# The first scores of one attention pair two products later, and the exponentials' tables loaded behind the last silu

## The chip, the cores and the metric

The kernel runs on one core of a Trainium2 chip. Its engines work side by side, each through its own list of instructions in order: TensorE (PE, matrix products into PSUM), VectorE (DVE), ScalarE (ACT), GpSimd (POOL), and SyncE (SP), which here issues the DMA transfers. The metric is the device time of one execution in microseconds (us); lower is better.

## The reference

An attention layer feeds a SwiGLU feed-forward layer, all in float32. There are 8 batches, 12 heads, 448 tokens and 64 features a head.

```python
def rmsnorm(x, g):
    rms = np.sqrt(np.mean(x * x, axis=-1, keepdims=True) + 1e-06)
    return x / rms * g
q_n, k_n = (rmsnorm(q, g_q), rmsnorm(k, g_k))
scores = scale * np.matmul(q_n, k_n.transpose(0, 1, 3, 2))   # scale = 1 / sqrt(64)
scores = scores - np.max(scores, axis=-1, keepdims=True)
attn = np.exp(scores)
attn = attn / (np.sum(attn, axis=-1, keepdims=True) + 1e-09)
attn = np.matmul(attn, v)
# heads side by side: x is 3584 tokens x 768
g = x @ w_gate                                # 768 x 1536
silu = g * (1.0 / (1.0 + np.exp(-g)))
out = (silu * (x @ w_val)) @ w_out            # 1536 x 768
```

## The kernel before, in words

**Tiling.** Attention is worked in 48 pairs of heads (`attention(m)`, m from 0 to 47). The feed-forward layer is worked in four blocks (`block(n)`, n from 0 to 3), each for two batches, that is, for twelve pairs. Pairs 0 to 11 come before block 0 (`EARLY` is 12). The later twelve of a group are interleaved with the block before them: pair 12 begins near the end of block 0's up stage, and pairs 12 to 23 fill the gaps of its down stage.

**A block.** The up stage makes `x @ w_gate` and `x @ w_val`. The matrices are cut in three by three pieces and multiplied with fifteen products (x0 to x14) of sums of pieces. Each step of the up stage is a product for the gate (w0, into a PSUM bank called `mm`) and one for the value (w1, into a bank called `at`), line L1472. Each bank has to be read (L1408, L1410, L1412, L1414: a copy on ACT or an addition or subtraction on DVE) before TensorE writes it again two products later. L1526 (`add_d`) is one more addition after x0. When a result of the gate is complete, ACT takes its silu (L1549), and DVE weighs the value with it (L1552). Lines L1184 and L1188 (`combined`) form sums of hidden pieces on DVE. The down stage (L1655) multiplies with `w_out` in the same manner.

**A pair.** Queries and keys are loaded (L768), squared on ACT (L807), summed on DVE (L838), and their inverse root is found by a logarithm and an exponential (L707, L708) with three small DVE steps (L713 to L715). POOL scales them (L888), DVE transposes them (L922), and ACT writes the queries with the gains (L925); a pair's scores can start after that. The scores (L970) come in four parts j: parts 0, 1 and 2 cover 896 columns, as two heads of 448, part 3 half as many. They go in the order 3, 0, 1, 2, into a ring of two PSUM banks called `st`, which the silus and the denominators share. Each part has its exponential on ACT (L985: tiles `es` for 0 to 2, `more` for 3). POOL adds the exponentials of 0 and 1 and then of 2 (L990); DVE adds part 3 (L996). PE multiplies the exponentials with the values (L1048) and sums them to a denominator (L1079); L1123 to L1151 turn that into a division.

**Order.** No engine chooses its order at run time. A planner (`Order`) takes pieces of work with `add(engine, us, when, emit, after, takes, uses, group, mode, early, rank)`. It plays the execution with assumed durations and writes out the instructions in the order in which it starts the pieces. `when` less `rank` is a piece's due time, by which pieces of one engine are sorted; `after` names pieces that must have ended; `takes` and `uses` name tiles in rings. `early`, if given, forbids a start earlier than `when - early`. On an engine, a piece that could start more than 0.4 us ahead of the one that is due goes first. A changed piece therefore can move other pieces, on any engine, for as long as the plan takes to fall into its old order.

**Tables.** ACT holds the table for one set of functions at a time. A piece with `mode="logarithms"` or `mode="silu"` is of one of two sets. When the planner starts a piece of another mode than the last piece with a mode on that engine, it adds 1.3 us to the plan; for logarithms (which include the exponentials) it also calls `load_tables` (L572), so that the load is written ahead of that piece. The load for the silus (shown at L1549) is put ahead of the first silu that needs it.

Of the kernel before, what the change touches and what calls it, by code (L numbers as in the profile page):

```python
# [364 lines left out]
class Order:  # L365
# [28 lines left out]
    def add(  # L394
        self, engine, us, when, emit, after=(), takes=(), uses=(), port=False, moves=(), group=None,
        mode=None, early=None, rank=0.0,
    ):
        piece = dict(
            engine=engine, us=us, when=when, emit=emit, takes=takes, port=port, moves=moves,
            group=group, mode=mode, early=early, rank=rank,  # L400
            after=[a for a in after if a is not None], end=None, n=len(self.pieces),
        )
        for tile_of in (*takes, *uses):
            self.users.setdefault(tile_of, []).append(piece)
        self.pieces.append(piece)
        return piece
# [87 lines left out]
def fast(  # L494
# [53 lines left out]
    NB = B // 2  # L548
# [5 lines left out]
    EARLY = 2 * NPAIR  # L554
# [116 lines left out]
    def block_start(n):  # L671
        return FIRST + n * (UP + BOTH) + MORE * (n > 0)

    def block_end(n):
        return block_start(n) + UP + MORE * (n == 0)

    def pair_time(m):
        if m < EARLY:
            return LEAD + m * PAIR, PAIR
        n, i = divmod(m - EARLY, EARLY)  # L680
        return block_end(n) + (i - 1) * BOTH / EARLY, BOTH / EARLY
# [54 lines left out]
    def attention(m):  # L736
# [8 lines left out]
        base, span = pair_time(m)  # L745

        ready = base - span
        early = m < EARLY
        rank = 60.0 if early else 0.0

        def add(*what, **more):
            return order.add(*what, rank=rank, **more)
# [31 lines left out]
        def load_values():  # L784
# [10 lines left out]
            early=4.0 if early else 25.0,  # L795
# [14 lines left out]
        for x in range(2):  # L810
# [4 lines left out]
                    after=[loaded[x], *squares, clusters.get("estimate") if m == 1 else None], uses=[("qk", (m, x))] + [("t", m)] * x,  # L815
# [41 lines left out]
        for x in range(2 if m < 2 else 0):  # L857
            sums = add(
                "DVE", 0.65, ready - 17.0, lambda x=x: summed_half(x),
                after=[squares[x], sums, clusters.get("turned") if x else None],  # L860
# [4 lines left out]
            after=squares, uses=[("t", m)], takes=[("ss", m)]  # L865
# [10 lines left out]
        def scale(x):  # L876
            if natural:
# [18 lines left out]
                after=[rr], port=True,  # L896
# [34 lines left out]
        if natural:  # L931
            of_turned = ("st", (m, "turned"))
            for xs_of in ((1, 0),) if m == 0 else ((1,), (0,)):
                qt = add(
                    "PE", 0.4 * len(xs_of), ready - 6.0, lambda xs_of=xs_of: [turn(x) for x in xs_of],
                    after=[scaled[1 - xs_of[-1]], qt], mode="full",
# [25 lines left out]
        def scores(j):  # L962
            st = take("st", (m, j), [P, 2, TB])
            n = S * width(j) // P
            for x in range(2):

                of_keys, of_queries = (x, 0) if j < NJ - 1 else (0, x)
                for h in range(2):
                    rows = ds(D * h, D)
                    nc.tensor.matmul(  # L970
                        st[ds(D * x, D), h, 0:n],
                        tiles["KT", m][rows, ds(P * j + D * of_keys, D)],
                        tiles["QT", m][rows, ds(Q * of_queries, n)],
                        start=True,
                        stop=True,
                    )


        def weights_of(j):
            return ("ea" if early else "e", (m, j)) if j < NJ - 1 else ("eh", m)  # L980

        def exps(j):
            e = take(*weights_of(j), [P, 2, S if j < NJ - 1 else Q])
            tiles["e", (m, j)] = e
            nc.scalar.activation(e, tiles["st", (m, j)][:, :, 0 : S * width(j) // P], AF.Exp)  # L985

        def add_up(j):
            to, e = tiles["sums", m], tiles["e", (m, j)]
            if j < NJ - 1:
                nc.gpsimd.tensor_tensor(  # L990
                    out=to, in0=tiles["e", (m, 0)] if j == 1 else to, in1=e, op=ALU.add
                )
            else:
                for x in range(2):
                    part = to[ds(D * x, D), :, ts(x, Q)]
                    nc.vector.tensor_tensor(out=part, in0=part, in1=e[ds(D * x, D)], op=ALU.add)  # L996
# [3 lines left out]
        ex, adds = {}, []  # L1000
        for j in (3, 0, 1, 2):
            before = clusters.get((m - 2, "weighted" if j in (3, 0) else "total"))
            when = (ready + 0.3 if j in (3, 0) else base) + 0.01 * (j % 3)
            half = j == NJ - 1
            st = add(
                "PE", 0.38 if half else 0.75, when, lambda j=j: scores(j),
                after=[kt, qt, staged.get(ES), before],
                uses=[("KT", m), ("QT", m)], takes=[("st", (m, j))],
                group=("c", m - 1 if j in (3, 0) else m), mode="quarters",
            )  # L1010
            ex[j] = add(
                "ACT", 0.54 if half else 0.92, when + 1.0, lambda j=j: exps(j),
                after=[st], uses=[("st", (m, j))],
                takes=[weights_of(j)], mode="logarithms",
            )
            if j in (1, 2) and not early:

                def more_sums(j=j):
                    if j == 1:
                        take("sums", m, [P, 2, S])  # L1020
                    add_up(j)

                adds.append(
                    add(
                        "POOL", 2.15, when + 2.0, more_sums, after=[ex[j], ex[0], *adds[-1:]],
                        port=True, uses=[("e", (m, j)), ("e", (m, 0)) if j == 1 else ("sums", m)],
                        takes=[("sums", m)] if j == 1 else [],
                    )
                )
# [57 lines left out]
        when = base + span * 0.8 if late else pair_time(m + 1)[0] + 0.1  # L1087
# [14 lines left out]
        for j in range(NJ):  # L1102
# [3 lines left out]
                after=[*ex.values(), load_v, last, clusters.get((m - 1, "total"))],  # L1106
# [331 lines left out]
    def block(n):  # L1438
        add = order.add
# [5 lines left out]


        value_banks = [("at", ("up", n, b)) for b in range(2)]
        free = {(0, 0): bank_read[0], (0, 1): bank_read[1], (1, 0): None, (1, 1): None}
        acc = {}

        def up_product(g, step, x, which, load, key):
            nonlocal last
            when = start + (2 * (15 * g + step) + which) * unit
# [12 lines left out]
            def emit():  # L1466
# [4 lines left out]
                for c in range(NC2):  # L1471
# [7 lines left out]
                after=[  # L1479
                    load, last, free[bank], *side_done[n, x],  # L1480
                    clusters.get((EARLY - 1, "weighted")) if opens and n == 0 else None,
                ],
# [10 lines left out]
            ready = value  # L1493
# [19 lines left out]
            if result == 2 and which:  # L1513
# [3 lines left out]
                emit_read, after=[last, acc.get((which, t)), *before], takes=takes,  # L1517
# [4 lines left out]
            if x == 0:  # L1522
# [12 lines left out]
                result, ready = 1, ("v2", (n, g, "t1"))  # L1535
# [6 lines left out]
            if result == 2:  # L1542
                ready = takes[0]
# [7 lines left out]
            def weigh():  # L1551
# [5 lines left out]
            gated = add(  # L1557
                "ACT", 0.55, when - 0.5, gate, after=[acc["gate", result]], takes=[act],
                mode="silu", rank=60.0 * (n == 0),
            )  # L1560
            hidden[g, result] = add(
                "DVE", 0.62, when + 1.0, weigh, after=[gated, done], uses=[act, ready],
                rank=60.0 * (n == 0),
# [14 lines left out]
        for g in range(NG):  # L1578
            steps = [(step, which) for step in range(15) for which in range(2)]
            if n == 0 and g == 0:  # L1580
                steps[: 2 * HEAD] = sorted(steps[: 2 * HEAD], key=lambda of: of[::-1])
            for step, which in steps:
                if step % 5 == 0 and which == 0:
                    key, load = up_load(g, step // 5)
                up_product(g, step, UP_ORDER[step], which, load, key)
        up_done[n] = last
        bank_read[:] = [free[0, 0], free[0, 1]]


# [27 lines left out]
        def step_time(x):  # L1617
            return block_end(n) + DOWN_ORDER.index(x) * span

        for g in range(NG):  # L1620
            when = start + 30 * (g + 1) * unit + 1.0
# [101 lines left out]
        for step, x in enumerate(DOWN_ORDER):  # L1723
            when = step_time(x)
            for s in range(2):
                down_product(step, x, s)
            after = {
                6: [(2, b3, b1, ALU.subtract, (1,))],
                1: [(3, h0, a3, ALU.add, (2, 10))],
                10: [(11, a3, b3, ALU.add, ()), (4, b2, b3, None, (2, 11))],  # L1730
                14: [(13, a2, b2, ALU.add, (2, 10))],
                2: [(12, h1, a1, ALU.subtract, (3,))],
                3: [(8, a3, b2, ALU.subtract, (12,)), (9, a2, a3, ALU.add, (6, 13))],
            }.get(x, [])
# [34 lines left out]
    for m in range(EARLY):  # L1769
        attention(m)  # L1770
# [12 lines left out]
    for n in range(NB):  # L1783
        block(n)
        for m in range(EARLY * (n + 1), min(NM, EARLY * (n + 2))):
            attention(m)
# [68 lines left out]
```

## Time and profile before

| | |
|---|---|
| median of 3 runs | 1458.52 us (1458.01 to 1459.07) |
| profiled execution | 1454.38 us |
| its span, first to last instruction | 1452.5 us |
| TensorE busy | 1424.2 us, 98% |
| VectorE busy | 881.2 us, 61% |
| ScalarE busy | 603.1 us, 42% |
| GpSimd busy | 400.7 us, 28% |
| granted TensorE clock, mean | 0.998 |
| the three costliest lines of TensorE | up products into `at` 401.2, into `mm` 400.4; scores 150.0 |

A line of the timeline has the start in us from the span's first instruction, the duration, the engine, the line of the kernel, the operation, what is written and what is read (partitions x elements), how many were taken together, and in brackets the idle time of that engine just before and what ended it. Several matmuls that follow each other are one line. The up stage of block 0 ends at about 318 us, those of blocks 1 and 2 at about 665 and 1013 us.

### The profile page before, as it was taken

The page shows a single profiled execution, that of the slowest core. Times are in us where ns is not written, and L with a number is a line of the kernel's source. Part 1 is how long each engine was busy: PE and PEld are TensorE (multiplying, and loading weights), DVE is VectorE, ACT ScalarE, POOL GpSimd, SP SyncE. Part 2 cuts the span into 40 slices and gives each one's busy share as a digit, 9 for nine tenths or more (in the row PEclk, how much of TensorE's full clock was granted, in tenths as well). Part 3 has the DMA queues.
Part 4 walks back from the last instruction along what each step waited for, and adds up shares of the span by engine and source line. Part 5 has one row for each costly group of instructions (what it writes and reads, how often), then busy time and mean ns, then how long its engine had stood idle before and what let it go on. Part 6 is the DMA issues. An engine that isn't in the chain of part 4 may idle for free.

```text
span 1452.5 us, 19359 instructions
## 1 busy us (share of the span) xinstructions
PE 1424.2 (98%) x6736; PEld 689.4 (47%) x6736; DVE 881.2 (61%) x1485; ACT 603.1 (42%) x1210; POOL 400.7 (28%) x476
## 2 busy tenths in 40 slices
PE   8999999989999999999999999999999999999997
PEld 4455454534444555544444455554444445555553
DVE  5889876888776434546877642455686644432533
ACT  6875444476553222455564122344655322122100
POOL 4756666634443000022343200011334300000000
PEclk9999999999999999999999999999999999999999
DMA  7777979854643433533543623443453452322235
GB/s 196 217 221 267 357 259 313 258 147 96 125 104 65 132 105 89 118 109 70 122 106 78 137 75 105 109 110 94 85 124 79 95 134 73 108 73 92 68 100 110
DMA packets 410416, 193.29 MB, mean 133 GB/s; under 512 B 280004, under 2 KB 390852, under 8 KB 410308
## 3 DMA queue, kind: packets, MB, share of 16 engines
q1 hardware_dynamic: 399040, 190.57, 48.7%
q10 hardware_dynamic: 11140, 1.38, 0.7%
q8 instruction: 55, 0.90, 0.3%
q14 instruction: 53, 0.43, 0.1%
q0 software_dynamic: 128, 0.00, 0.0%
HBM read 157.29 MB, written 34.60 MB: 132 GB/s over the span
## 4 chain that ended last, share of the span: by engine, by line
PE 92%; DVE 2%; ACT 2%; DMA 2%; issue 1%; POOL 1%; SPq 0%; DVEq 0%; ACTq 0%; POOLq 0%
PE at L1472 25%; PE mm L1472 24%; PE mm L1655 24%; PE st L970 8%; PE at L1048 8%; PE st L1079 1%; PE mm L1079 1%; DMA out_dram<-spare 1%; PE st L908 1%; PE mm L1748 1%; ACT es L985 1%; DMA work<-in_q_dram 0%; DVE work L916 0%; SPq L768 0%; ACT work L918 0%
## 5 line engine op out<-in xcount | busy, mean ns | idle before, releaser
L1472 PE MATMUL at<-xs,ws 128*128 128x448 f32 x960 | 401.2, 540 | 5.1 <-DVE v L1412 4.0
L1472 PE MATMUL mm<-xs,ws 128*128 128x448 f32 x960 | 400.4, 540 | 0.2 <-DVE hs L1314 0.2
L1472 PEld LDWEIGHTS at<-xs,ws 128*128 128x128 f32 x960 | 181.4, 190 | 187.3 <-issue 166.7
L1472 PEld LDWEIGHTS mm<-xs,ws 128*128 128x128 f32 x960 | 181.9, 190 | 180.3 <-issue 178.6
L888 POOL TENSOR_TENSOR work<-work,rr 128x448 f32<-128x448 f32 x72 | 66.5, 943 | 473.9 <-DVE rr L715 225.6
L1655 PE MATMUL mm<-gt,ws 128*128 128x448 f32 x448 | 175.5, 543 | 0.0
L970 PE MATMUL st<-work 64*64 64x448 f32 (+1 forms) x1536 | 150.0, 499 | 10.8 <-ACT work L918 4.7
L1410 DVE TENSOR_TENSOR gt<-gt,mm 128x448 f32<-128x448 f32 x64 | 39.8, 621 | 189.0 <-PE mm L1472 162.6
L985 ACT ACTIVATE es<-st 128x896 f32<-128x896 f32 x129 | 114.0, 915 | 95.1 <-PE at L1048 82.6
L1655 PE MATMUL mm<-hs,ws 128*128 128x448 f32 x384 | 151.0, 544 | 0.0
L990 POOL TENSOR_TENSOR sums<-es 128x896 f32<-128x896 f32 x36 | 76.9, 2136 | 176.5 <-PE st L1079 117.2
L1655 PEld LDWEIGHTS mm<-gt,ws 128*128 128x128 f32 x448 | 83.6, 190 | 83.4 <-issue 80.4
L1549 ACT ACTIVATE st<-gt 128x448 f32<-128x448 f32 x96 | 52.3, 547 | 158.1 <-DVE gt L1414 85.4
L1408 ACT COPY gt<-mm 128x448 f32<-128x448 f32 x80 | 42.6, 532 | 157.8 <-PE mm L1472 157.7
L1048 PE MATMUL at<-es,v 64*64 64x448 f32 (+1 forms) x1032 | 106.0, 507 | 0.0
L1655 PEld LDWEIGHTS mm<-hs,ws 128*128 128x128 f32 x384 | 71.4, 190 | 71.5 <-issue 70.4
L970 PEld LDWEIGHTS st<-work 64*64 64x64 f32 x1536 | 51.1, 132 | 77.7 <-issue 36.2
L1408 ACT COPY v<-at 128x448 f32<-128x448 f32 x96 | 51.0, 531 | 81.8 <-PE at L1472 81.1
L990 POOL TENSOR_TENSOR sums<-sums,es 128x896 f32<-128x896 f32 x36 | 76.2, 2117 | 2.8
L1048 PEld LDWEIGHTS at<-es,v 64*64 64x64 f32 (+1 forms) x1032 | 44.1, 134 | 56.2 <-issue 50.4
L1410 DVE TENSOR_TENSOR v<-v,at 128x448 f32<-128x448 f32 x64 | 39.8, 621 | 40.3 <-PE at L1472 39.8
L1552 DVE SCALAR_TENSOR_TENSOR gt<-st,v 128x448 f32<-128x448 f32 x96 | 59.7, 622 | 7.0
(170 smaller groups left out, 1553.4 us busy)
## 6 DMA issues: line engine op xcount, KB each, us to landing
ws<-up_sides SPq DMA_DIRECT2D x32, 1024.0 KB, 5.6
ws<-down_sides SPq DMA_DIRECT2D x16, 1024.0 KB, 5.7
ws<-down_sides SPq DMA_DIRECT2D x28, 512.0 KB, 4.5
ws<-up_sides SPq DMA_DIRECT2D x16, 768.0 KB, 4.9
out_dram<-spare SPq DMA_DIRECT2D x168, 56.0 KB, 2.1
v<-in_v_dram SPq DMA_DIRECT2D x96, 96.0 KB, 2.4
ws<-up_sides SPq DMA_DIRECT2D x32, 256.0 KB, 5.9
ws<-up_sides SPq DMA_DIRECT2D x16, 512.0 KB, 5.8
```

What stands on the lines that cost most here:

```text
L888: nc.gpsimd.tensor_tensor(out=tiles["t", m][:, x], in0=tiles["qk", (m, x)], in1=rr.to_broadcast([P, NC, C]), op=ALU.mult,)
L970: nc.tensor.matmul(st[ds(D * x, D), h, 0:n], tiles["KT", m][rows, ds(P * j + D * of_keys, D)], tiles["QT", m][rows, ds(Q * of_queries, n)] ...
L985: nc.scalar.activation(e, tiles["st", (m, j)][:, :, 0 : S * width(j) // P], AF.Exp)
L990: nc.gpsimd.tensor_tensor(out=to, in0=tiles["e", (m, 0)] if j == 1 else to, in1=e, op=ALU.add)
L1048: nc.tensor.matmul(tiles["at", (m, x)][ds(D * h, D), ds(0, Q) if early else queries], tiles["v", m][rows, j, h], tiles["e", (m, j)][rows, ...
L1079: nc.tensor.matmul(to[ds(D * h + C * x, C)], halves[:, x] if half else many[:, 0:C], term[:, h, 0:Q] if half else term[:, h, ts(x, Q)], st ...
L1408: nc.scalar.copy(to, ps)
L1410: nc.vector.tensor_tensor(out=to, in0=old, in1=ps, op=ALU.add)
L1472: nc.tensor.matmul(ps(), w[:, which, c, at], xs[:, SLOT[x], c], start=fresh and c == 0, stop=c == NC2 - 1, skip_group_check=True,)
L1549: nc.scalar.activation(take(*act, [P, 2, TB])[:, 0, 0:S], to, AF.Silu)
L1552: nc.vector.scalar_tensor_tensor(to, tiles[act][:, 0, 0:S], 1.0 / SCALE, tiles[ready], op0=ALU.mult, op1=ALU.mult,)
L1655: nc.tensor.matmul(banks[s][:, 0:S], w[:, s, g, at], where[x][:, g], start=fresh and g == 0, stop=g == NG - 1, skip_group_check=True,)
```

## The change

Three pieces of code change, all of them arguments for the planner; no instruction's operands change.

- For pair 12 alone, the due time of score parts 3 and 0 becomes 13 us later, and these two may not start before it (`early=0.0`). Parts 1 and 2 of that pair keep theirs, as do all other pairs.
- Each block collects its silu pieces in `gates`.
- After the products of each up stage but the last block's, an ACT piece of 0 us that emits nothing is added. It has `mode="logarithms"` and comes after all silus of that block, with a due time of half a us before the block's end less a rank of 60. When the planner starts it, `load_tables` is called if the last mode was silu.

```diff
         for j in (3, 0, 1, 2):
             before = clusters.get((m - 2, "weighted" if j in (3, 0) else "total"))
-            when = (ready + 0.3 if j in (3, 0) else base) + 0.01 * (j % 3)
+            when = (ready + 0.3 + (13 if m == EARLY else 0.0) if j in (3, 0) else base) + 0.01 * (j % 3)
             half = j == NJ - 1
             st = add(
                 "PE", 0.38 if half else 0.75, when, lambda j=j: scores(j),
                 after=[kt, qt, staged.get(ES), before],
                 uses=[("KT", m), ("QT", m)], takes=[("st", (m, j))],
                 group=("c", m - 1 if j in (3, 0) else m), mode="quarters",
+                early=0.0 if m == EARLY and j in (3, 0) else None,
             )
...
         value_banks = [("at", ("up", n, b)) for b in range(2)]
+        gates = []
         free = {(0, 0): bank_read[0], (0, 1): bank_read[1], (1, 0): None, (1, 1): None}
...
                 "ACT", 0.55, when - 0.5, gate, after=[acc["gate", result]], takes=[act],
                 mode="silu", rank=60.0 * (n == 0),
             )
+            gates.append(gated)
...
         up_done[n] = last
+        if n < NB - 1:
+            add(
+                "ACT", 0.0, block_end(n) - 0.5, lambda: None, after=gates, mode="logarithms",
+                rank=60.0,
+            )
         bank_read[:] = [free[0, 0], free[0, 1]]
```

## The prediction

> **What bounds the kernel now.** I read the page's busy times first: TensorE (PE) is busy 1424.2 of 1452.5 us, 98%, so the end moves only if one of PE's few gaps closes or opens, or if a new one appears. Next comes the list of what PE waits for, whose columns are the wait, total us, times, longest us:
>
> ```profile
> PE 1424.2 (98%) x6736; PEld 689.4 (47%) x6736; DVE 881.2 (61%) x1485; ACT 603.1 (42%) x1210; POOL 400.7 (28%) x476
> ...
> PE at L1472 <- DVE v L1412: 4.0, 2, 3.0
> PE st L970 <- ACT work L925: 2.6, 1, 2.6
> ...
> PE st L970 <- ACT es L985: 1.8, 6, 0.4
> ...
> PE st L1079 <- ACT more L985: 0.7, 2, 0.4
> ```
>
> Two of these, 2.6 and 3.0 us, lie within 11 us of each other at the end of block 0's up stage, where pair 12's first scores stand. The timeline there, in us from the span's start:
>
> ```profile
> 295.01 1.36 PE L970 MATMUL st<-work 64*64 64x224 f32 x16 [2.56 <-ACT work L925]
> 296.31 1.77 PE L1472 MATMUL mm<-xs,ws 128*128 128x448 f32 x4
> 298.01 1.74 PE L970 MATMUL st<-work 64*64 64x448 f32 x16
> 299.31 0.62 DVE L1188 TENSOR_TENSOR hs<-gt,hs 128x448 f32<-128x448 f32 x1
> 300.05 2.39 POOL L990 TENSOR_TENSOR sums<-es 128x896 f32<-128x896 f32 x1 [2.07 <-ACT es L985]
> 300.50 2.43 DVE L1188 TENSOR_TENSOR hs<-gt,hs 128x448 f32<-128x448 f32 x1
> 302.52 2.34 POOL L990 TENSOR_TENSOR sums<-sums,es 128x896 f32<-128x896 f32 x1
> 302.85 2.49 DVE L1526 TENSOR_TENSOR gt<-gt,w 128x448 f32<-128x448 f32 x1
> 305.26 0.61 DVE L1412 TENSOR_TENSOR v<-v,at 128x448 f32<-128x448 f32 x1
> 305.92 1.77 PE L1472 MATMUL at<-xs,ws 128*128 128x448 f32 x4 [2.98 <-DVE v L1412]
> ```
>
> The reader is to see a chain. PE's last product waits until DVE has read the bank "at" (L1412, 305.26). That read stands behind two DVE additions that take 2.43 and 2.49 us where the same form took 0.62 at 299.31. Both long ones coincide with the two POOL sums of pair 12's exponentials (L990). So the 2.98 us stall is set by POOL starting 0.45 us before DVE's second L1188.
>
> The third place is the end of blocks 1 and 2. Block 1:
>
> ```profile
> 664.01 0.55 ACT L1549 ACTIVATE st<-gt 128x448 f32<-128x448 f32 x1 [2.46 <-DVE gt L1412]
> 667.87 0.53 ACT L1408 COPY v<-mm 128x448 f32<-128x448 f32 x1 [3.31 <-PE mm L1655]
> 669.56 0.67 ACT L925 ACTIVATE work<-work,gg 128x448 f32<-128x448 f32 x1 [1.16 <-PE st L970]
> 670.25 1.28 ACT L572 ACT_TABLE_LOAD   x1
> 671.54 1.73 ACT L985 ACTIVATE es<-st 128x896 f32<-128x896 f32 x2
> 672.51 0.61 PE L970 MATMUL st<-work 64*64 64x224 f32 x8 [0.39 <-ACT es L985]
> 673.32 0.98 PE L970 MATMUL st<-work 64*64 64x448 f32 x8 [0.20 <-ACT es L985]
> ```
>
> The table load stands between L925 and the exponentials that PE waits for, although ACT was idle 3.31 us after the last silu. Block 2 shows the same: silu 1012.06, load 1018.30, PE waits 0.38 and 0.20.
>
> **What the Trainium skill says.** "SBUF — State Buffer", section "Who interferes with whom": a DVE instruction with two SBUF inputs contends with a GpSimd instruction that reads SBUF, and whichever starts first holds the shared port for its whole length. The trace agrees: 0.62 us alone, 2.43 and 2.49 beside L990. It also agrees on the order: DVE's L714, starting level with an L990 at 328.51, took 0.19; L715, 0.05 us behind another at 340.54, took 2.09. "ScalarE: Activation LUTs", section "What ACT_TABLE_LOAD costs": about 1283 ns, plus a drain of about 1380. The trace has the 1.28, but the next exponential starts 0.01 us after the load ends, so I take 1.28 and no drain.
>
> **Part (a): pair 12's turns.** The built order of the changed program has, on PE, score j1, product x0 w0, then j3, j0, j2, then x0 w1, x5 w0, x5 w1; before it was j3, j0, x0 w0, j1, j2, x0 w1 and so on. No instruction is added or removed. ACT takes the exponentials as j1, j3, j0, j2.
>
> Step 1. The first score still needs the queries that L925 writes, whichever j it is: the wait of 2.56 us stays, and PE starts at 295.01. Nothing gained.
>
> Step 2. j1 alone is 8 matmuls of 448. j3 and j0 (224 and 448) took 1.30 us together and j1 with j2 (twice 448) 1.66, so one 448 is 0.83 to 0.92. Product x0 w0 starts at 295.84 to 295.93, 0.38 to 0.47 earlier than 296.31. Its DVE reader L1412 started 1.80 us after it (296.31 to 298.11): now at 297.70 to 297.73, as DVE's L922 (297.11, 0.65) lets it. The second L1188 was 2.39 us behind that L1412: now 300.09 to 300.12 instead of 300.50.
>
> Step 3. j3 starts when x0 w0 is out, 1.70 us after it: 297.54 to 297.63. In the trace its exponential starts 0.68 after the score and j0's 1.42 to 1.48 after: 298.96 to 299.11, ending 0.92 later, and POOL's first sum starts 0.07 after that end (299.98 to 300.05 before): 299.95 to 300.10. It needs the exponentials of j0 and j1, and j0's is now the later of the two. So POOL's start hardly moves from 300.05.
>
> Step 4. DVE's second L1188 therefore arrives 0.02 to 0.14 us behind POOL instead of 0.45. By the 0.05 us example above it is still blocked: L1188, L1526 and the bank's read stay where they were, and PE's stall with them, give or take 0.15. That is the value I take. The other end is that DVE gets the port first: see the first rival.
>
> Step 5. j2's score waits for the exponential of j3 (a ring of two banks): some 0.15 us, and x0 w1 starts at about 299.8 instead of 299.67. It costs nothing while PE stands 2.98 us later on; without that stall it costs the 0.15.
>
> Step 6. Exponentials of pair 12 no longer crowd ACT early, and the square L807 (0.58 us) slips from before the silu load (305.42, ahead of which ACT idles 3.71) to behind the L925 at 307.66. That delays the following log table load and exponentials by at most 0.58. The last silu (317.48) ended 0.84 before DVE took it up at 318.87 (two L1552, to 320.0), and PE's turn that needs the bank so freed came at 321.23, 1.2 later. These two covers hide it: priced at nothing; without them 0.58.
>
> Step 7. The planner reorders block 0's down stage on ACT, DVE, POOL and the DMA queue of SP; on PE only pair 12's denominator (L1079) moves one product back, and the scores or denominators of pairs 14 and 17 change places with a product. The same instructions, so the price is waits alone. Before, PE idles only 0.41 us in that stage; the same stage of blocks 1 and 2, planned apart, idles 1.60 and 0.95. So 0 to +1.2; below, -0.4 if the one wait goes. I take +0.3. No weight load (ws) on SP moves to a place where a product would wait for it.
>
> **Part (b): the load behind the silu.** As many loads as before (26). Block 0's end already had the load right behind the last silu (318.05), so nothing changes there. In blocks 1 and 2 the 1.28 us move into the 3.31 us idle after the silu. Behind L925 the exponentials start at 670.25 instead of 671.54; the first ends at about 671.15, before PE is ready for the next scores at 672.12. So 0.39 and 0.20 vanish, 0.59 us, and 0.38 and 0.20 in block 2. The denominator (L1079) and the product follow 0.59 earlier. What is late next is at 686.83, 0.37 us for "more" (L985), which stands on ACT behind L848 and two exponentials; those wait for PE's own reading, so most of the gain passes, but the logarithm at 682.84 hangs on a chain of DVE and POOL and may hold back up to 0.35. I take 0.5 for each block: -1.0; ends -0.3 and -1.3.
>
> Sum against the profiled execution's 1454.38 (1452.5 of span and 1.88 around it): -0.15 + 0.3 - 1.0 = -0.85, so 1453.5. The median of the runs is 4.14 us above that execution; the same change on it gives 1458.52 - 0.85, about 1457.6.
>
> **Rivals.**
> - DVE wins the port. A few hundredths decide step 4. Then the second L1188 takes 0.62, only L1526 is held (until POOL's first sum ends near 302.5), the bank is read at about 303.0 and the last product starts at about 303.7 instead of 305.92: -2.2. With +0.3 and -1.0 it is -2.9, so 1455.6. For it: the distance shrinks from 0.45 to at most 0.14. Against: every estimate of the distance is above zero.
> - Down stage worse. Twelve pairs take turns in block 0's down stage, and a pair whose exponentials come late costs what blocks 1 and 2 show at their ends, 0.59. If eight pairs do so (4.7 us) with the -1.0 kept, it is +3.6, so 1462.1; slower by 0.2% from seven on. For it: every queue but PE's is reordered there, and DVE is busier there than in the other two (77% of 318 to 480 us, against 72% of 664 to 830). Against: PE's order is nearly unchanged, and its idle of 0.41 us in 162 says that inputs came in time; one of them followed by hand, pair 12's division (L1151), still ends about 1.2 us ahead of its reader.
> - No effect. The 0.59 of each block is taken back at later waits set by DMA or DVE (763 to 769 in block 1, where a wait of 0.44 hangs on an incoming transfer), and the port race is lost: +0.3, 1458.8.
>
> **How the numbers follow.** About 0.2%, 2.9 us, is what a measurement can tell here. Chances: main case 0.48, DVE wins 0.23, down stage worse 0.10, no effect 0.19. DVE's win lies on the boundary, so half of it counts as faster, with 0.06 from the low tail of the main case (down stage -0.4, blocks -1.3, and a partial shift of the stall): 0.18. The slower case reaches beyond the boundary in most of its 0.10: 0.08. Same: 0.74. The range covers main, no effect and most of DVE's win: from 1455.2 to 1459.2; the main case's own is 1456.7 to 1459.0.
>
> **What would show it.** Right: the wait of 2.56 us at the first score still there; the wait at the last product still near 2.9, with a long DVE L1188 beside a POOL L990; no PE wait on exponentials at some 672 and 1020 us, with a table load right behind the silu. Rival one: an L1188 of 0.62 with POOL's sum close behind it, and a wait under 1 us. Rival two: new waits for L985 or at L1079 between 330 and 480 us. I am wrong if the first scores start earlier than 295.0, if the POOL sums start clearly later than 300.1, or if the up stages shift elsewhere.

## The result and the profile after

The changed kernel takes 1455.53 us (median of 16 runs, 1452.85 to 1456.79), the kernel before, in 16 runs beside it, 1457.49 (1456.07 to 1459.87). The ratio of the means (1455.11 and 1457.70) is 0.9982, with a 95% interval of 0.9976 to 0.9989: 2.6 us faster (1.6 to 3.5). The forecast was 0.9 us faster, with a range that reached from 1455.2 to 1459.2.

The waits of TensorE in the changed kernel's profile (total us, times, longest; line numbers are up to 8 higher than before):

```profile
PE st L970 <- ACT work L925: 2.6, 1, 2.6
PE st L1080 <- ACT more L985: 1.7, 4, 0.5
...
PE at L1474 <- DVE v L1413: 1.4, 2, 1.0
...
PE st L970 <- ACT es L985: 0.8, 4, 0.2
```

The 2.6 us at the first score (the first gap, below) are still there. The stall of 2.98 us at the last product (the second gap) is not: its line fell from 4.0 to 1.4. The waits for exponentials fell from 1.8 to 0.8, those of the denominator rose from 0.7 to 1.7. The timeline at the end of block 0's up stage:

```profile
295.19 0.98 PE L970 MATMUL st<-work 64*64 64x448 f32 x8 [2.56 <-ACT work L925]
296.11 3.07 PE L1474 MATMUL mm<-xs,ws 128*128 128x448 f32 x4
299.11 2.60 PE L970 MATMUL st<-work 64*64 64x224 f32 x24
...
301.60 0.62 DVE L1189 TENSOR_TENSOR hs<-gt,hs 128x448 f32<-128x448 f32 x1
...
301.88 2.34 POOL L990 TENSOR_TENSOR sums<-es 128x896 f32<-128x896 f32 x1 [3.72 <-ACT es L985]
302.14 2.56 DVE L1528 TENSOR_TENSOR gt<-gt,w 128x448 f32<-128x448 f32 x1
...
305.29 1.77 PE L1474 MATMUL at<-xs,ws 128*128 128x448 f32 x4 [0.38 <-DVE v L1413]
```

DVE's second L1189 (L1188 before) is 0.28 us ahead of POOL's sum and takes 0.62; only L1528 is held. So the last product waits 0.38. That is the first rival's picture, but not by its cause: POOL is late (301.88, forecast 299.95 to 300.10), and so, by less, is DVE (301.60, forecast 300.09 to 300.12), for product x0 w0 takes 3.07 us where it took 1.77. The table of stretches shows why. Its columns are the stretch, its length, the busy times of PE, PEld, DVE, ACT and POOL with instruction counts, then the granted TensorE clock, the share of the DMA engines and GB/s. Before:

```profile
296.00:298.00 2.00, 2.00 (x8) 0.68 (x4) 0.65 (x2) 1.15 (x2) 1.84 (x2) 1.00 0.85 204
298.00:300.00 2.00, 2.00 (x18) 0.81 (x18) 1.85 (x4) 0.94 (x2) 0.00 (x0) 1.00 0.71 114
```

After:

```profile
296.00:298.00 2.00, 2.00 (x7) 0.97 (x4) 0.82 (x2) 0.92 (x1) 1.69 (x2) 0.61 1.00 286
298.00:300.00 2.00, 2.00 (x14) 0.67 (x16) 0.79 (x2) 0.00 (x0) 0.15 (x1) 0.54 0.67 107
300.00:302.00 2.00, 2.00 (x21) 0.53 (x14) 1.93 (x4) 1.66 (x3) 0.12 (x1) 1.00 0.50 92
```

TensorE ran at half its clock for a while; the trace's record of the clock puts this spell from 296.43 to 299.85, 3.413 us. Such a spell had no place in the forecast, and a large part of the experiments is about it.

The other part, the table loads, went as written. Block 1 after, with the table load behind the silu:

```profile
664.28 0.55 ACT L1551 ACTIVATE st<-gt 128x448 f32<-128x448 f32 x1 [2.46 <-DVE gt L1413]
664.84 1.28 ACT L572 ACT_TABLE_LOAD   x1
...
670.64 1.73 ACT L985 ACTIVATE es<-st 128x896 f32<-128x896 f32 x2
...
672.21 1.31 PE L970 MATMUL st<-work 64*64 64x224 f32 x16
...
673.99 0.59 PE L1080 MATMUL st<-sums,many 128*32 128x224 f32 x8 [0.46 <-ACT more L985]
```

The two waits of 0.39 and 0.20 are gone and the scores run through. A new wait of 0.46 stands at the denominator: ACT now does the four L848 copies (0.88) ahead of `more`. Block 2 shows the same.

### The profile page after: what moved, and what is told of

Read it like the earlier page. It is cut to its first block, busy times and chain, and to the rows that moved or that the text cites. A ratio compares the mean times of both kernels' runs of the same rounds, so it can differ in the third digit from the quotient of the medians.

```text
span 1452.0 us, 19362 instructions
## 1 busy us (share of the span) xinstructions
PE 1426.0 (98%) x6736; PEld 689.5 (47%) x6736; DVE 879.8 (61%) x1485; ACT 601.6 (41%) x1210; POOL 405.7 (28%) x476
## 4 chain that ended last, share of the span: by engine, by line
PE 90%; DMA 3%; DVE 2%; ACT 2%; SPq 1%; issue 1%; POOL 1%; ACTq 0%; DVEq 0%; POOLq 0%
PE at L1474 25%; PE mm L1474 25%; PE mm L1663 23%; PE at L1049 8%; PE st L970 7%; PE st L1080 1%; PE mm L1080 1%; DMA out_dram<-spare 1%; SPq L768 1%; DMA work<-in_k_dram 1%; ACT es L985 1%; DMA xs<-in_moe_w_gate_dram 0%; PE st L908 0%; DMA v<-in_v_dram 0%; ACT work L918 0%
## 5 line engine op out<-in xcount | busy, mean ns | idle before, releaser
L888 POOL TENSOR_TENSOR work<-work,rr 128x448 f32<-128x448 f32 x72 | 71.8, 1016 | 467.5 <-DVE rr L715 341.6
```

Source lines behind the costliest of these rows:

```text
L888: nc.gpsimd.tensor_tensor(out=tiles["t", m][:, x], in0=tiles["qk", (m, x)], in1=rr.to_broadcast([P, NC, C]), op=ALU.mult,)
```

## The experiments

Times are ratios to the kernel before, run on the same chip, with 95% intervals. For stages I use the stretches between the first products of the stages in each trace: "up 0" is from the first up product (123.41 before) to the first down product (318.13), and so on; "down 1 to down 2" is from the first down product of block 1 to the end of block 2's down stage. "The race" is that of POOL's first sum of pair 12 and DVE's second L1188 for the port that they share.

**Part (a) alone (e1), part (b) alone (e2).** Each is the diff above less the other's lines.

> Part (a) alone: pair 12's score parts 3 and 0 later, no table piece. Theory A (the stall at the last product of block 0's up stage is what was saved: DVE's second L1188 now goes ahead of POOL's first sum): wait at that product under 1 us, L1188 at 0.62 us, and the kernel 1.5 to 2.5 us faster than before (2.6 for the stall less about 0.6 that block 0's down stage loses by the other order). Theory B (the gain is that of the table loads in blocks 1 and 2): within 0.7 us of before.

> Part (b) alone: tables loaded behind the last silu, pair 12 as before. Theory A: 0.5 us in each of blocks 1 and 2, about 1.0 us faster than before, with the stall of 2.6 to 3.0 us at the last product of block 0's up stage still there. Theory B: 2 to 2.6 us faster, the whole of the difference.

Measured: (a) 0.9998 (0.9989 to 1.0006); (b) 0.9986 (0.9978 to 0.9994). The two multiply to 0.9984, against 0.9982 for both. So theory A failed for (a), which was to give 1.5 to 2.5 us: pair 12's turns bring nothing that can be measured, and in the timed runs the tables carry the gain. Their 2.0 us have an interval of 0.9 to 3.2, which holds theory A's 1.0 as well as theory B's 2 to 2.6. In the profile of (a), the race was lost:

```profile
294.65 1.23 PE L970 MATMUL st<-work 64*64 64x448 f32 x8 [2.56 <-ACT work L925]
295.81 3.17 PE L1473 MATMUL mm<-xs,ws 128*128 128x448 f32 x4
298.91 2.25 PE L970 MATMUL st<-work 64*64 64x224 f32 x24
...
301.33 2.13 POOL L990 TENSOR_TENSOR sums<-es 128x896 f32<-128x896 f32 x1 [3.73 <-ACT es L985]
301.40 2.54 DVE L1189 TENSOR_TENSOR hs<-gt,hs 128x448 f32<-128x448 f32 x1
...
306.94 1.40 PE L1473 MATMUL at<-xs,ws 128*128 128x448 f32 x3 [2.57 <-DVE v L1413]
```

L1189 is 0.07 us behind POOL and held, and the last product waits 2.57. There was a half-clock spell here too, but from 295.25 to 298.67: it ended before parts 3 and 0 began at 298.91.

**The POOL sums exchanged (e3).** The kernel before, its order unchanged on every engine; for pair 12 alone both sums are written where the second stood:

```diff
-                    out=to, in0=tiles["e", (m, 0)] if j == 1 else to, in1=e, op=ALU.add
+                    out=to, in0=tiles["e", (m, 0)] if j == (2 if m == EARLY else 1) else to, in1=e, op=ALU.add
...
-                    add_up(j)
+                    if m != EARLY:
+                        add_up(j)
+                    elif j == 2:
+                        add_up(2)
+                        add_up(1)
```

> The kernel before, with the same plan and order on every engine, except that pair 12's first POOL sum adds parts 0 and 2 of the exponentials and the second adds part 1, so that POOL cannot start before part 2's exponential ends (301.25 instead of 299.98). If the stall of 2.98 us is the port's doing: DVE's second L1188 takes 0.62, L1526 is at most held by one sum, the last product waits 0 to 1 us instead of 2.98, 2 to 3 us faster than before. If the stall had another cause: no change beyond 0.5 us.

```profile
301.33 0.62 DVE L1192 TENSOR_TENSOR hs<-gt,hs 128x448 f32<-128x448 f32 x1
301.87 0.62 DVE L1530 TENSOR_TENSOR gt<-gt,w 128x448 f32<-128x448 f32 x1
...
302.15 2.34 POOL L990 TENSOR_TENSOR sums<-es 128x896 f32<-128x896 f32 x1 [5.00 <-ACT es L985]
302.40 0.61 DVE L1416 TENSOR_TENSOR v<-v,at 128x448 f32<-128x448 f32 x1
...
303.61 1.67 PE L1476 MATMUL at<-xs,ws 128*128 128x448 f32 x4
```

Both additions take 0.62, the last product waits for nothing, and the kernel is at 0.9968 (0.9955 to 0.9981), 4.7 us faster. So the port, and who is first at it, made the stall; this is shown. It is more than the 2 to 3 us expected. In the traces up 0 is 3.3 us shorter (193.05 against 196.35, each with a spell). The mean clock was higher too, 0.9977 against 0.9966 of before beside it, which by the fit below is worth 1.2. Closing the stall takes away the second gap, after which a spell can come (below); that this raised the clock is likely, not shown.

**The gap filled.** The changed kernel, with matmuls of no use (the scores overwrite what they give) in the 2.56 us ahead of pair 12's first score; six in the first of these (e4), three in the second (e5):

```diff
+            if m == EARLY and j == 1:
+                for _ in range(3):
+                    nc.tensor.matmul(
+                        st[:, 0, 0:S], ident[:, 0:P], xs[:, SLOT[5], 0], start=True, stop=True,
+                    )
```

> The changed kernel, with six matmuls of no use (128x128 by 128x448, overwritten by the scores) ahead of pair 12's first score, which fill 2.25 of the 2.56 us in which TensorE stands idle there. In the profile of the changed kernel TensorE ran at half its clock for 3.4 us right after that gap, and product x0 w0 took 3.07 us instead of 1.77, which put POOL's first sum at 301.88, behind DVE's L1188. Theory C (the half clock is what let DVE win): at full clock the sum starts near 300.1 to 300.2, L1188 is held (over 2 us), the last product waits 2.5 to 3 us, and the kernel is 1.5 to 2.5 us slower than the changed one. Theory D (DVE wins at full clock as well): x0 w0 takes 1.77, L1188 0.62, the last product waits 1 us or less, and the time is that of the changed kernel or 0 to 0.5 lower.

> The changed kernel with three idle matmuls instead of six ahead of pair 12's first score (six overran the gap: the score began at 297.09 instead of 295.19). Three take about 1.2 us of the 2.56 and should leave the score where it was, near 295.2, without half clock. Theory C (at full clock POOL's sum is first): first sum near 300.1, second L1188 0.02 to 0.14 us behind it and held over 2 us, the last product of the up stage waits about 2.6 us; the time is within 1 us of the changed kernel, since a half-clock spell, worth 1.2 to 1.6 us, is saved in nearly every execution and a stall of 2.2 us is had in every one. Theory D (DVE is first at full clock too): wait under 1 us, 1 to 2 us faster than the changed kernel.

Both expectations price a call at half of what it takes: in the trace each call is two matmuls, 0.38 us apart. With six the clock stayed whole, but their twelve matmuls, begun at 292.49 right behind the last product, ran past the gap: the score began at 297.09, so that the ratio of 0.9999 (0.9990 to 1.0008) holds some 2 us of their own. The race is clean all the same:

```profile
298.00 1.77 PE L1479 MATMUL mm<-xs,ws 128*128 128x448 f32 x4
299.70 2.25 PE L975 MATMUL st<-work 64*64 64x224 f32 x24
...
302.12 2.13 POOL L995 TENSOR_TENSOR sums<-es 128x896 f32<-128x896 f32 x1 [3.96 <-ACT es L990]
302.20 2.54 DVE L1194 TENSOR_TENSOR hs<-gt,hs 128x448 f32<-128x448 f32 x1
...
307.73 0.64 PE L1479 MATMUL at<-xs,ws 128*128 128x448 f32 x1 [2.57 <-DVE v L1418]
```

At full clock POOL is first by 0.08 us, and the stall is there. With three (2.42 us, then 0.31 idle), the score was on time, and POOL was first by 0.20 (299.23 against 299.43; DVE had stood 0.17 for a DMA), with a wait of 2.58; the ratio was 0.9991 (0.9983 to 1.0000), 1.3 us slower than the changed kernel's where at most 1 was expected, though the intervals overlap. Theory C holds: at full clock the changed kernel loses the race. A half-clock spell followed here as well, at 306.24, behind the stall of 2.58.

**More executions.** The changed kernel twice more (e9, e10), and the kernel before once more (e11), unchanged, one run each, for the traces (1455.93, 1454.62 and 1455.85 us).

> The changed kernel once more, for another profiled execution. Theory C': the race at DVE's second L1188 is won only where a half-clock spell of 3.41 us is still running when score parts 3 and 0 of pair 12 are computed, which puts the exponential of part 0, and so POOL's sum, later than product x0 w0's reader. Then L1188 takes 0.62 and the last product waits under 1 us. With no spell, or one that ends before part 3 starts, L1188 is held over 2 us and the wait is near 2.6. Rival: the race falls either way without regard to the spell.

> The changed kernel again, a third profiled execution; as for the second: a wait under 1 us at the up stage's last product if and only if a half-clock spell overlaps the scores of parts 3 and 0, else near 2.6.

> The kernel before once more. Theory C': its profile of before happened to have no half-clock spell near 295 us, while most executions have one, at one of its two gaps; where there is one, the stretch from pair 12's first score to the up stage's last product is 12.5 us instead of 10.9, and the stall of 2.6 to 3.0 us is there in either case. Rival: no spell in this execution, or a stall under 1 us with one.

In both of the changed kernel's, the spell ended before parts 3 and 0 began (295.26 to 298.67 with part 3 at 299.29; 294.97 to 298.38 with part 3 at 298.68), POOL was first by 0.07 and 0.08, and the wait was 2.58 and 2.59. The second:

```profile
295.63 3.12 PE L1474 MATMUL mm<-xs,ws 128*128 128x448 f32 x4
298.68 2.26 PE L970 MATMUL st<-work 64*64 64x224 f32 x24
...
301.10 2.14 POOL L990 TENSOR_TENSOR sums<-es 128x896 f32<-128x896 f32 x1 [3.73 <-ACT es L985]
301.18 2.55 DVE L1189 TENSOR_TENSOR hs<-gt,hs 128x448 f32<-128x448 f32 x1
...
306.73 1.02 PE L1474 MATMUL at<-xs,ws 128*128 128x448 f32 x2 [2.59 <-DVE v L1413]
```

Only in the first execution did the spell (to 299.85) run into parts 3 and 0 (from 299.11); that put part 0's exponential 1.77 us behind the start of part 3 (300.88 less 299.11) where it is 1.43 in the other five, and so POOL behind DVE. The long product alone doesn't do it: e1, e9 and e10 had 3.17, 2.80 and 3.12 us for it and lost, for DVE's additions and the scores of parts 3 and 0 both wait for that product. Of the six executions with part (a)'s turns and the sums as they were (after, e1, e4, e5, e9, e10), one won the race, and it is the one whose spell overlapped those scores. Before's new execution had its stall of 3.00, and a spell not at the first gap but behind the second, from 306.71 (my expectation of 12.5 us from first score to last product was for a spell at the first; there it was 10.9).

**The parts together.** Tables with the exchanged sums; both parts with the exchanged sums; tables, sums and three filling matmuls (at part 3, which is first there).

> Part (b) with the exchanged POOL sums, pair 12's turns as before. If the two are independent: 0.9 us for the tables and 3.5 to 4.6 us for the sums, together 4.5 to 5.5 us faster than before, 2 to 3 us faster than the changed kernel. If they share a gain: no better than the exchanged sums alone, about 4.6.

> The changed kernel with the exchanged POOL sums, so that the port race is decided for DVE at any clock. If part (a) gives only the race, and costs 0.6 us or more in block 0's down stage by its split turns: slower than tables and sums without part (a), by 0.5 to 1.5 us, and 1 to 3 us faster than the changed kernel. If part (a) gives something else as well: level with or faster than tables and sums without it.

> Tables and exchanged sums, with three idle matmuls ahead of pair 12's first score against the half clock. If the half-clock spell after the 2.56 us gap costs TensorE 1.2 to 1.6 us in most executions even where no stall follows: another 1.0 to 1.5 us faster than tables and sums alone, and the mean granted clock 0.001 higher. If the spell is had by most executions at another place anyway: no difference.

| kernel | ratio to before | interval | mean of the runs, us | mean granted clock |
|---|---|---|---|---|
| tables, sums (e6) | 0.9973 | 0.9963 to 0.9984 | 1452.88 | 0.9976 |
| turns, tables, sums (e7) | 0.9981 | 0.9974 to 0.9988 | 1454.30 | 0.9976 |
| tables, sums, filled (e8) | 0.9963 | 0.9949 to 0.9976 | 1451.54 | 0.9988 |
| before, beside these | 1 | | 1456.84 | 0.9968 |

With the race decided by the sums, pair 12's turns are a loss: 1454.30 against 1452.88 at the same mean clock. Nor is e7 faster than the changed kernel (0.9981 and 0.9982), where 1 to 3 us were expected. Its trace shows a reason: POOL's second sum now meets a later addition of DVE, and two scores wait for what stands behind it on DVE, 1.5 us together.

```profile
302.80 2.08 POOL L990 TENSOR_TENSOR sums<-sums,es 128x896 f32<-128x896 f32 x1
302.95 2.42 DVE L1532 TENSOR_TENSOR v<-v,v 128x448 f32<-128x448 f32 x1
...
306.24 0.61 PE L970 MATMUL st<-work 64*64 64x224 f32 x8 [0.86 <-DVE gt L1558]
...
307.50 0.98 PE L970 MATMUL st<-work 64*64 64x448 f32 x8 [0.65 <-DVE gt L1558]
```

In e3 and e6 that addition began 0.22 and 0.18 us ahead of the second sum and took 0.62 and 0.61. So the exchange decides one meeting at the port, and in this execution another was lost.

The filled one has 0.0012 more clock than the one not filled and is 1.3 us faster on the means, as expected, though over 5 and 10 runs only. It beats both kernels: a median of 1451.55 against 1457.24 of before beside it, 0.9963 where the changed kernel has 0.9982. Tables and sums gave 3.9 us, less than the 4.5 to 5.5 of independent parts. The tables added to the sums bring no gain over the sums alone that these runs can show (0.9973 and 0.9968, with intervals that overlap).

## Why the prediction was wrong

**The step that failed.** The sum has no term for the granted clock. Steps 2 to 4 take their times from one execution in which it was whole at both gaps, and the base takes the 4.14 us between that execution and the median as fixed. The runs show a half-clock spell near one of the gaps in most executions. It costs about 1.6 us itself. Where it ran over the scores of parts 3 and 0, step 4's stall did not stay: its term of -0.15 became -2.1 against a kernel before with a spell (up 0 took 194.21 and 196.35), and -0.5 against the profile that I had, without one (194.72). Where it ended sooner, the term was -0.2 (196.12 against 196.35), as forecast. A second term, step 7's +0.3, was too small: it came to 0.6 to 1.4. How the 2.6 us of the timed runs divide between these is in part open (below).

**Stage by stage.** The first products of the stages give (us):

| execution | up 0 | down 0 | down 1 to down 2 | stall at last product |
|---|---|---|---|---|
| before, no spell at the first gap | 194.72 | 161.19 | 509.66 | 2.98 |
| before again (e11), spell at the second gap | 196.35 | 161.19 | 509.99 | 3.00 |
| (b) alone (e2), spell at the first | 196.35 | 161.20 | 509.38 | 2.97 |
| changed, race won | 194.21 | 161.79 | 508.90 | 0.38 |
| changed (e9), race lost | 196.12 | 162.55 | 508.53 | 2.58 |
| changed (e10), race lost | 196.13 | 162.31 | 508.07 | 2.59 |
| (a) alone (e1), race lost | 196.11 | 162.42 | 509.39 | 2.57 |
| sums (e3), spell at the first | 193.05 | 161.20 | 510.18 | none |
| turns, tables, sums (e7), no spell | 193.33 | 162.27 | 508.05 | none |
| tables, sums, filled (e8), no spell | 192.32 | 161.19 | 509.01 | none |

**Step 1 was right**: 2.56 us at the first score in every one of them.

**Steps 2 to 4 hold where no spell lies over parts 3 and 0.** DVE behind POOL by 0.02 to 0.14 was forecast; it was 0.08 with six filling matmuls, 0.20 with three, and 0.07 to 0.08 in e1, e9 and e10, whose spell ended sooner. The stall of the lost race is 2.58 where I left 2.98 less 0.15: 0.4 gained, of which up 0 keeps 0.2. What failed is the premise of step 3, that the scores of parts 3 and 0 always run at full clock. The one race that was won had the first rival's signs, and one that I had named for being wrong, POOL's sums clearly later than 300.1; its cause, the half clock, is in neither case. In 8 of the 10 profiled executions whose first gap was not filled, a half-clock spell stands near one of the two gaps. A spell costs about 1.6 us: up 0 takes 196.35 with it and 194.72 without, the stall being the same. The profile I worked from was one of the two without.

**Why a gap of 2.56 us does that.** The Trainium skill, "TensorE: Matmul & The Clock Gate", section "Part 1: The HAM clock gate (the "warmup" mystery)", says that the clock falls to half after an idle window of 3413 ns, and that the windows run free of the kernel. The traces agree on length and grid: each such spell is 3.413 us, and the full-clock stretch ahead of it is 290.133 us in six of them, 85 windows. They differ on idle: no gap here fills a window. In the changed kernel's window before the spell, 293.02 to 296.43, TensorE worked from 295.19, 1.24 us or 36%. Worked out so from the matmul records for the windows around both gaps, those followed by a spell had 25 to 41%, and those with 46% or more had none. (The ends of matmuls are modelled, so the shares are rough.) A window far from the gaps, in e6 from 24.86 to 28.28, had 43% and was followed by a spell as well. Filling the first gap (e4, e5, e8) left no spell there in all three. So where the windows fall decides whether a gap of 2.6 us costs another 1.6, and here also who is first at the port.

**Step 7 was mis-sized.** Block 0's down stage was to lose 0.3 (up to 1.2). It lost 0.60 with the race won, and 1.1 to 1.4 in the three executions above with it lost. Part of it is seen directly: before, pair 17's scores of parts 3 and 0 (366 us) stood in one turn of 1.24 us; now they are in two turns, 0.54 and 0.91, and 0.2 to 0.6 us of waits for exponentials come near 422 us, in e9 and e10 another 0.57 and 0.21 near 383. So rival two had the right place, at less than a third of its price of 4.7, and in a lost race it eats more than the stall gives: (a) alone is 0.9998.

**Part (b) was right, in size and in place.** 0.5 us a block was forecast. From the first down product of block 1, and of block 2, to the product behind the denominator, all four executions without the tables take 10.09 us, and all nine with them 9.57 or 9.58 (before: 664.66 to 674.75; changed: 664.92 to 674.50). That is 0.51 to 0.52 a block, 1.0 in all. The whole stretch is 1.2 shorter (508.5 on the mean of the three changed executions, 509.7 of before, before again and (a) alone), but single executions scatter by 0.8 there. Alone, without (a), the trace of e2 shows only some 0.3 to 0.6, since in its order block 2's up stage takes 186.03 instead of 185.34, with waits of 0.28 and 0.20 for exponentials, while the timed runs show 2.0 (0.9 to 3.2). The difference in block 0's end was nothing, as said.

**The base was wrong too.** I put the 4.14 us between the profiled execution and the median down as a constant. It isn't one: over 205 runs of these kernels (a straight line, with a level for each kernel on each chip) the time falls by 1.15 us (0.08) for each 0.001 of mean clock. Before's 83 runs beside the experiments have a mean of 0.9967, the changed kernel's 16 have 0.9972. That would be 0.6 us of the measured difference, an estimate, for the clocks of the 16 runs of before in that comparison are not on record. There is other scatter too: the stretch ahead of the first up product, where the change moves nothing, took 122.33 to 125.10 us in the 13 traces. At equal clock the fit has the changed kernel 1.3 to 1.6 us faster than before, (b) alone 0.9 and (a) alone 0.0, each to about 0.3.

**What stays open.** How often the race is won in timed runs isn't known; one of three profiled executions of the changed kernel won it, and a win is worth 1.9 us in up 0 (194.21 against 196.12) and 0.5 to 0.8 in down 0. The changed kernel had 1 of 16 runs with a clock of 0.996 or less, (a) alone 5 of 14, though they share block 0's order: whether that is chance was not tried. So of 2.6 us, 1.0 is shown by the traces to be the tables'; about 0.6 goes with a higher clock, by the estimate above; and the rest, about 1, lies within what won races and the runs' scatter can give, which is not shown.

## What to carry to other kernels

Where two engines start within 0.1 us of each other at a shared port, don't forecast the winner: put the later one behind something it truly needs, as the exchanged sums do (0.9968): in all four executions with them both additions took 0.62 us. Then see what the delayed one meets next (2.42 us in e7). A short gap of TensorE can cost more than its length, so look at the granted clock in the stretch behind each gap of 2 us and more, and in more than one execution, before using durations from it. A turn that is moved can have a price where it no longer shares a turn with its neighbours (0.54 and 0.91 us instead of 1.24 for pair 17); count turns as well as instructions.

## What the runs showed of the hardware

- A window of 3.413 us in which TensorE worked 25 to 43% of the time was followed by 3.413 us of half clock (weight loads 0.34 us instead of 0.19, a product 3.07 instead of 1.77); windows with 46% and more, around the two gaps, were not. The windows' grid lies differently against the program from run to run.
- DVE with two operands in SBUF, starting 0.07 us after POOL's sum, took 2.54 to 2.55 us instead of 0.62; starting 0.28 us before it, 0.62, and the sum then took 2.34 where it took 2.13 or 2.14 with DVE behind it.
